# A mixing product of seven by seven block products: when its outer sums and their loads are placed, step by step

## The chip, the cores and the metric

The kernel runs on one core of a Trainium2 chip. TensorE (PE) multiplies, VectorE (DVE) and ScalarE (ACT) work on tiles, GpSimd (POOL) and SyncE (SP) issue DMAs, which 16 DMA engines carry out. The metric is the device time of one execution in microseconds, as the median of several runs.

## The reference

Three networks follow each other; the change lies in the middle one, in the product with `w_spatial`:

```python
h = np.maximum(x @ w_in, 0.0)                     # x: 4 batches, 3072 positions, 256
u, v = h[..., :512], h[..., 512:]
v_n = (v - mean(v)) / np.sqrt(var(v) + 1e-06)
v_s = np.einsum('ts,bsd->btd', w_spatial, v_n) + b_spatial[None, :, None]   # 3072 x 3072
x2 = (u * v_s) @ w_out
r = np.maximum(x2 @ w2_in, 0.0)
out = (s * (r * r) + b) @ w2_out
```

All of it is in float32.

## The kernel before

The program has three stages: `attention`, which also makes `v_n`; `mixing`, which multiplies `w_spatial` with `v_n`; and `output`.

**Products of products.** `mixing` computes a matrix product by Strassen's method in Winograd's form, on two levels. On the outer level there are seven products of a sum of blocks of `w_spatial` (called a) with a sum of blocks of `v_n` (called b). They run in the order of `OUTER`, and are called the first to the seventh outer product here. The second and the fourth have an outer sum on both sides whose result is also kept in DRAM for a later product, the fifth has one on a, the sixth one on both, the seventh one on b; the first and third have none. Each outer product is in turn seven inner products, called passes, in the order of `INNER` (2, 5, 3, 1, 6, 7, 4). A pass has six steps, 0 to 5, one for each strip of 128 rows that are summed over. So an outer product has 42 steps, and the stage 294. A step is 24 matmuls: four groups `d` of 128 columns of b, three products of high and low halves (float32 is split into two parts of fewer bits), two halves of a.

**What stands in memory.** Four quarters of a (`a11`, `a12`, `a21`, `a22`) and of b, each in six strips, have fixed tiles. A quarter of the next outer product is loaded into its tile once the last use of the old one is past (`LAST`, `freed`), on SP's queue. Where the outer product has a sum, the second operand goes into a staging tile, `st_a` or `st_b`, three buffers each, and VectorE adds it (`add`, L786); a result that is kept is stored by a DMA on POOL's queue (L788). A load pair is the tile and its staging tile.

**A step of the program.** The order is written out by hand and each engine works in order. At step n the loop in `run` issues:

- `multiply(n)`, 24 matmuls
- `high` for step n+2: two casts on ScalarE (L845)
- `sums(n + 3)`: the inner sums, on VectorE: none in passes 1, 4 and 7 of the order; one of a and one of b in the second; two of a in the third; three of b in the fifth (L831 to L833); one of a in the sixth (L836). As they are issued three steps ahead, they fall three steps before their pass
- at the last step of a pass `evacuate` for groups 0 and 1: an add of the result to a kept tile on VectorE after passes 4, 5, 6 and 7 (L885, "kept add") and a copy on ScalarE after passes 1, 2, 3 and 6 (L889, "kept copy")
- `low` for step n+2: two subtractions on VectorE (L849), the low halves
- `evacuate` for groups 2 and 3
- outer sums that are due, a conversion if n is in `CONVERSIONS`, and new loads

A group's accumulator has one buffer, so the first matmuls of a pass on it wait until the kept add or copy of the pass before is done.

**Conversions.** Forty times a half of a weight of the last stage, which comes as 64-bit numbers, is converted to two parts: ten operations on VectorE (L143 to L158), one cast on ScalarE (L155) that waits for VectorE's L149, and a store on POOL (L161). They use the same staging buffers: the raw data and the result are `st_a` tiles. The raw data is loaded by SP (L128) ahead of the conversion.

**Before the change** a sum's load is issued as soon as its tile is free and a staging buffer is left (`loads`), and the sum is taken three steps later (`outer_sums(3)`). At a conversion all sums that are open are taken at once (`outer_sums(0)`), so that the staging buffers are free.

Of the kernel before, what the change touches and what calls it, by code (L numbers as in the profile page):

```python
# [27 lines left out]
NS = TQ // 128  # L28
# [140 lines left out]
class Chains:  # L169
# [5 lines left out]
    def add(self, stages):  # L175
        stages[0]()
        rest = list(stages[1:])
        if rest:
            self.live.append(rest)
        return rest  # L180
# [47 lines left out]
def attention(tc, nc, x, w_r, w_i, b_r, b_i, c_f, c_b, c_g, c_v, c_s, zd, vd, yd, vn, chunks, cd, follow, nb=NB):  # L228
# [491 lines left out]
FIRST_USE = {"a12": 0, "b21": 0, "a21": 1, "a22": 1, "b12": 1, "b11": 1, "a11": 2, "b22": 2}  # L720
# [1 line left out]


CONVERSIONS = {42 * g + 6 * p + i for g, p, i in (
# [8 lines left out]


class Stage:
# [6 lines left out]
def mixing(tc, nc, ws, vn, md, sd, convert_half):  # L742
# [10 lines left out]
    def place(pool, names):  # L753
        for name in names:
            n = TQ if name[0] == "a" else 512
            for i in range(NS):
                q[name, i] = pool.tile([128, n], F32, tag=f"{name}{i}", name=name)
# [4 lines left out]
    def source(what, name, i):  # L762

        x, y = int(name[1]) - 1, int(name[2]) - 1
        if what[0] == "w":
            return ws[2 * what[1] + x, (2 * what[2] + y) * NS + i]
        if what[0] == "v":
            return vn[2 * what[2] + y][(2 * what[1] + x) * NS + i]
        return sd[what[0]][x, y, i]

    added = []
    now = [0]

    def load(g, name, i):
        first, then = OUTER[outer[g]][0 if name[0] == "a" else 2:][:2]
        t = q[name, i]
        nc.sync.dma_start(out=t, in_=source(first, name, i))
        if then is None:
            return
        op, second, kept = then  # L780
        n = t.shape[1]
        s = banks[2].tile([128, n], F32, tag="st_" + name[0], name="st_" + name[0], bufs=3)
        nc.sync.dma_start(out=s, in_=source(second, name, i))

        def add():
            nc.vector.tensor_tensor(out=t, in0=t, in1=s, op=getattr(ALU, op))  # L786
            if kept:
                nc.gpsimd.dma_start(out=sd[kept][int(name[1]) - 1, int(name[2]) - 1, i], in_=t)  # L788
        added.append((now[0], name[0], add))

    todo = []

    def loads(taken):

        n = {"a": 3 - taken, "b": 3}
        for _, kind, _ in added:
            n[kind] -= 1
        for x in sorted(todo):
            g, _, i, name = x
            if OUTER[outer[g]][1 if name[0] == "a" else 3] is not None:  # L800
                if n[name[0]] <= 0:
                    continue
                n[name[0]] -= 1
            todo.remove(x)
            load(g, name, i)

    def outer_sums(age):
        while added and added[0][0] <= now[0] - age:
            added.pop(0)[2]()

    sub, add = nc.vector.tensor_sub, nc.vector.tensor_add
    term, hl = {}, {}

    def sums(n):

        p, i = INNER[n // NS % 7], n % NS
        a11, a12, a21, a22, b11, b12, b21, b22 = (q.get((x, i)) for x in QUARTERS)
        if p == 2:
            a, b = a12, b21
        elif p == 5:  # L820
            add(a21, a21, a22)
            sub(b12, b12, b11)
            a, b = a21, b12
        elif p == 3:
            sub(a21, a21, a11)
            a, b = ring.tile([128, TQ], F32, tag="s4", name="s4", bufs=2), b22
            sub(a, a12, a21)
        elif p == 1:
            a, b = a11, b11
        elif p == 6:  # L830
            sub(b12, b22, b12)  # L831
            sub(b11, b12, b11)  # L832
            sub(b22, b21, b12)  # L833
            a, b = a21, b12
        elif p == 7:
            sub(a21, a22, a21)  # L836
            a, b = a21, b11
        else:
            a, b = a22, b22
        term["a", n], term["b", n] = a, b  # L840

    def high(kind, n):
        t = term[kind, n]
        s = hl[kind, n] = ring.tile([128, 2, t.shape[1]], F32R, tag=kind + "_hl", name=kind + "_hl", bufs=3)
        nc.scalar.copy(s[:, 0, :], t)  # L845

    def low(kind, n):
        s = hl[kind, n]
        sub(s[:, 1, :], term.pop((kind, n)), f(s)[:, 0, :])  # L849

    def freed(n):
        g, at = divmod(n // NS, 7)
        if g + 1 < len(outer):
            todo.extend((g + 1, FIRST_USE[x], n % NS, x) for x, last in LAST.items() if last == at)
# [4 lines left out]
    def multiply(n):  # L859
        p, i = INNER[n // NS % 7], n % NS  # L860
        a, b = hl.pop(("a", n)), hl.pop(("b", n))
        fresh = p in (2, 5, 1, 4)
        for d in range(4):
            if i == 0 and fresh:
                acc[d] = banks[0].tile([128, 2, 512], F32, tag=f"acc{d}", name="acc")
            for c, (m, w) in enumerate(PASSES):
                for h in range(2):
                    nc.tensor.matmul(acc[d][:, h, 0:TH], b[:, m, d * 128:(d + 1) * 128], a[:, w, h * TH:(h + 1) * TH],  # L868
                                     start=fresh and i == 0 and c == 0, stop=i == NS - 1 and c == 2,
                                     skip_group_check=True)  # L870
# [6 lines left out]
    def evacuate(n, d):  # L877
        g, at = divmod(n // NS, 7)
        p = INNER[at]
        ps = acc[d][:, :, 0:TH]  # L880
        out = {1: (2, 0, 0), 6: (3, 0, 1), 7: (5, 1, 1), 4: (0, 1, 0)}.get(p)
        if out is not None:
            k, x, y = out
            t = kept.pop((k, d))
            add(t, ps, t)  # L885
            nc.gpsimd.dma_start(out=md[outer[g]][x, y, d], in_=t.rearrange("p h t -> p (h t)"))
        if p in (2, 5, 3, 7):
            t = kept[{7: 0}.get(p, p), d] = keep_tile({2: 0, 5: 1, 3: 2, 7: 0}[p], d)
            nc.scalar.copy(t, ps)  # L889
# [10 lines left out]
    def split_first():  # L900
        n = begun[0]
        begun[0] += 1
        sums(n)
        for kind in "ab":
            high(kind, n)
            low(kind, n)

    def run():
        banks.append(left("m_acc", 1, space=PSUM))
        banks.append(right("m_keep", 1))  # L910
        place(left("m_a11", 1), ("a11",))
        banks.append(left("m_stage", 2))
        stage = banks[2]
        while begun[0] < 2:
            split_first()
        while first:
            _, i, x = first.pop(0)
            load(0, x, i)
        sums(2)
        conversion = []  # L920
        for n in range(total):
            now[0] = n
            multiply(n)
            ends = n % NS == NS - 1
            if n + 2 < total:
                high("a", n + 2)
                high("b", n + 2)
            if n + 3 < total:
                sums(n + 3)
            if ends:  # L930
                evacuate(n, 0)
                evacuate(n, 1)
            if n + 2 < total:
                low("a", n + 2)
                low("b", n + 2)
                freed(n + 2)
            if ends:
                evacuate(n, 2)
                evacuate(n, 3)
            outer_sums(3)  # L940
            if n in CONVERSIONS:
                outer_sums(0)
                conversion.pop()()
            loads(len(conversion))
            if not conversion and any(m in CONVERSIONS for m in range(n + 1, n + 5)):
                conversion.append(convert_half(stage))
        left.close()
        right.close()
# [227 lines left out]
def network(ctx, tc, ins, out):  # L1176
# [25 lines left out]
    with tc.manual_schedule():  # L1202
        attention(tc, nc, ins['x'], ins['w_r'], ins['w_i'], ins['b_r'], ins['b_i'],
                  ins['c_f'], ins['c_b'], ins['c_g'], ins['c_v'], ins['c_s'], zd, vd, yd, vn, chunks, cd,
                  lambda: mixing(tc, nc, ins['moe_w_spatial'], vn, md, sd, convert_half)).run()
        output(tc, nc, yd, md, chunks, cd, ins['moe_b_spatial'], ins['moe2_s'], ins['moe2_b'], out)
# [25 lines left out]
```

## Time and profile before

| | us |
|---|---|
| median of 3 runs | 3177.33 (3176.37 to 3178.32) |
| the profiled execution | 3178.05 |
| its span, first to last instruction | 3176.3 |
| TensorE busy | 3076.6 (97%) |
| VectorE busy | 2309.0 (73%) |
| first and last matmul of `mixing` start at | 539.9 and 1809.9 |

The profile is one execution. The shares are over the whole span. A matmul's record is longer than the time until the next one starts, since matmuls are pipelined; the time of a step is read from the starts of its matmuls. A row of windows below gives the stretch and its length, then busy time and count of PE, PE's weight loads, DVE, ACT and POOL, the granted TensorE clock (1.00 is full speed), the busy share of the DMA engines and the GB/s they moved.

### The profile page before, as it was taken

Reading aid. Unit: us, or ns where it says so; the run is one execution under the profiler, and the core shown is the slowest. Engines: PE = TensorE matmul, PEld = TensorE weight load, DVE = VectorE, ACT = ScalarE, POOL = GpSimd, SP = SyncE. Lnnn points to the kernel's source line nnn. Section 1 sums busy time; section 2 is a strip of 40 time slices with the busy share of each in tenths; the row PEclk is TensorE's granted clock in tenths of the full one; section 3 lists DMA queues with packets and bytes.
Section 4 is the critical chain, followed back from the end, with each engine's and each line's share of the span. In section 5 each row is a group of like instructions: output and inputs, shape, how many; then the busy total and the mean of one; then the engine's idle time right before and its main releaser. Section 6 shows DMA issues by size and latency. Waiting matters only on the chain.

```text
span 3176.3 us, 46578 instructions
## 1 busy us (share of the span) xinstructions
PE 3076.6 (97%) x17960; PEld 3004.5 (95%) x17960; DVE 2309.0 (73%) x3495; ACT 1429.3 (45%) x2244; POOL 420.1 (13%) x537
## 2 busy tenths in 40 slices
PE   6999997999999999999999999999999999999999
PEld 5888986999999899999999989999999999999999
DVE  5888998798878788788888755656565656656564
ACT  5777766433344343434344334444444444444443
POOL 2665534021101200000000100000000000000000
PEclk8999999999999999999999999999999999999999
DMA  8987767586537947375562712111111111110110
GB/s 245 290 285 237 244 215 276 194 337 253 187 138 258 393 147 268 107 258 191 167 211 67 260 63 75 45 45 53 55 65 56 65 56 65 55 65 31 67 45 16
DMA packets 222839, 488.32 MB, mean 154 GB/s; under 512 B 22356, under 2 KB 106136, under 8 KB 222616
## 3 DMA queue, kind: packets, MB, share of 16 engines
q1 hardware_dynamic: 186344, 343.03, 32.0%
q0 software_dynamic: 36272, 142.31, 12.3%
q8 instruction: 141, 2.31, 0.3%
q14 instruction: 82, 0.67, 0.1%
HBM read 322.72 MB, written 162.53 MB: 153 GB/s over the span
## 4 chain that ended last, share of the span: by engine, by line
PE 57%; DVE 5%; ACT 1%; issue 1%; DMA 0%; SPq 0%; ACTq 0%; DVEq 0%
PE ps_h L1073 17%; PE oacc L1094 17%; PE acc L868 15%; PE ps_o L1054 4%; PE ps_u L1036 4%; DVE a_hl L849 1%; DVE kept L885 1%; DVE b_hl L849 1%; DVE b L831 0%; DVE b L833 0%; DVE a L786 0%; DVE b L832 0%; DVE m L1004 0%; ACT kept L889 0%; ACT a_hl L845 0%
## 5 line engine op out<-in xcount | busy, mean ns | idle before, releaser
L868 PE MATMUL acc<-a_hl,b_hl 128*128 128x384 f32 x7056 | 1239.1, 336 | 31.3 <-DVE kept L885 18.1
L868 PEld LDWEIGHTS acc<-a_hl,b_hl 128*128 128x128 f32 x7056 | 1231.4, 189 | 38.9 <-issue 11.0
L1073 PE MATMUL ps_h<-x_hl,w 128*128 128x384 f32 x3072 | 582.4, 337 | 1.5 <-ACT x_hl L1057 0.9
L1094 PE MATMUL oacc<-q_hl,w 128*128 128x384 f32 x3072 | 575.5, 336 | 0.6 <-DVE q_hl L1080 0.6
L1073 PEld LDWEIGHTS ps_h<-x_hl,w 128*128 128x128 f32 x3072 | 544.9, 188 | 2.1 <-ACT x_hl L1057 1.3
L1094 PEld LDWEIGHTS oacc<-q_hl,w 128*128 128x128 f32 x3072 | 537.1, 188 | 0.9 <-DVE q_hl L1080 0.8
L845 ACT CAST a_hl<-a 128x768 fp32r<-128x768 f32 x253 | 211.7, 837 | 512.4 <-PE acc L868 420.2
L1080 DVE TENSOR_TENSOR q_hl<-r,q_hl 128x768 fp32r<-128x768 f32 x256 | 245.4, 959 | 230.7 <-ACT q_hl L1079 230.7
L1078 DVE TENSOR_TENSOR r<-r 128x768 f32<-128x768 f32 x256 | 244.9, 957 | 205.9 <-ACT r L1077 205.9
L1079 ACT CAST q_hl<-r 128x768 fp32r<-128x768 f32 x256 | 213.7, 835 | 301.6 <-DVE r L1078 301.6
L1077 ACT ACTIVATE r<-ps_h 128x768 f32<-128x768 f32 x256 | 208.3, 814 | 312.4 <-PE ps_h L1073 309.1
L849 DVE TENSOR_TENSOR a_hl<-a,a_hl 128x768 fp32r<-128x768 f32 x253 | 241.6, 955 | 126.4 <-ACT a_hl L845 125.8
L849 DVE TENSOR_TENSOR b_hl<-b,b_hl 128x512 fp32r<-128x512 f32 x295 | 202.4, 686 | 0.0
L845 ACT CAST b_hl<-b 128x512 fp32r<-128x512 f32 x295 | 181.7, 616 | 0.1
L578 PE MATMUL ps_vp<-win,y_hl 128*128 128x512 f32 x576 | 149.9, 396 | 1.5 <-ACT y_hl L478 1.2
L1036 PE MATMUL ps_u<-y_hl,w 128*128 128x384 f32 x768 | 145.7, 339 | 1.8 <-DVE y_hl L1022 1.8
L1054 PE MATMUL ps_o<-g,w 128*128 128x384 f32 x768 | 139.4, 337 | 1.6 <-DVE g L1044 1.0
L1036 PEld LDWEIGHTS ps_u<-y_hl,w 128*128 128x128 f32 x768 | 135.5, 190 | 3.1 <-DVE y_hl L1022 2.1
L1054 PEld LDWEIGHTS ps_o<-g,w 128*128 128x128 f32 x768 | 133.6, 188 | 2.5 <-DVE g L1044 1.6
L885 DVE TENSOR_TENSOR kept<-acc,kept 128x768 f32<-128x768 f32 x112 | 103.1, 953 | 23.7 <-PE acc L868 22.4
L578 PEld LDWEIGHTS ps_vp<-win,y_hl 128*128 128x128 f32 x576 | 101.2, 189 | 20.1 <-ACT y_hl L478 1.6
L1043 ACT CAST g<-m 128x768 fp32r<-128x768 f32 x64 | 53.5, 836 | 143.6 <-DVE m L1039 143.6
(140 smaller groups left out, 3722.2 us busy)
## 6 DMA issues: line engine op xcount, KB each, us to landing
a<-in_moe_w_spatial_dram SPq DMA_DIRECT2D x144, 384.0 KB, 4.8
b<-vn SPq DMA_DIRECT2D x168, 256.0 KB, 5.4
md<-kept POOLq DMA_DIRECT2D x112, 384.0 KB, 4.9
m<-md SPq DMA_DIRECT2D x56, 768.0 KB, 6.1
st_a<-in_moe_w_spatial_dram SPq DMA_DIRECT2D x72, 384.0 KB, 6.1
vn<-vr POOLq DMA_DIRECT2D x96, 256.0 KB, 4.5
s<-a POOLq DMA_DIRECT2D x48, 384.0 KB, 6.0
x_f<-in_x_dram SPq DMA_DIRECT2D x32, 384.0 KB, 6.9
```

The lines of the kernel that those rows point to most:

```text
L578: nc.tensor.matmul(ps, y[:, a, k, o:o + 128], win[k][:, w, :], start=c == 0, stop=c == 5)
L845: nc.scalar.copy(s[:, 0, :], t)
L849: sub(s[:, 1, :], term.pop((kind, n)), f(s)[:, 0, :])
L868: nc.tensor.matmul(acc[d][:, h, 0:TH], b[:, m, d * 128:(d + 1) * 128], a[:, w, h * TH:(h + 1) * TH], start=fresh and i == 0 and c == 0, st ...
L1036: nc.tensor.matmul(ps[:, d, 0:TH], win[k][:, a, o:o + 128], y[:, w, k, :], start=c == 0, stop=c == 5)
L1054: nc.tensor.matmul(ps[:, h, 0:TH], wo[k // 2][:, a, o:o + 128], g[:, w, k, :], start=c == 0, stop=c == 11)
L1073: nc.tensor.matmul(ps[:, e, 0:TH], w[:, a, o:o + 128], x[:, i, j, :], start=c == 0, stop=c == 5)
L1077: nc.scalar.activation(r, ps[:, :, 0:TH], AF.Relu)
L1078: nc.vector.tensor_mul(r, r, r)
L1079: nc.scalar.copy(s[:, 0], r)
L1080: nc.vector.tensor_sub(s[:, 1], r, f(s)[:, 0])
L1094: nc.tensor.matmul(ps[:, h, 0:TH], w[:, a, o:o + 128], s[:, i, e, :], start=ff == 0 and c == 0, stop=ff == 2 * NP - 1 and c == 2)
```

## The change

It alters when outer sums, their loads and the conversions are issued; the work itself is the same, operation by operation, and TensorE's order is unchanged.

- Each quarter has a fixed place for its sum, `ADD_AT`, in steps from the start of the outer product ahead of the one that uses it; strip i follows i steps later. 18 is the start of the fourth pass, 30 of the sixth, 36 of the seventh; 42 is the start of the outer product itself, 45 the middle of its first pass and 48 the start of its second.
- A load that belongs to a sum is issued at the earliest `LEAD`, three, steps before that place, if a staging buffer is left.
- At a conversion all open sums are still taken. The table of conversions has 40 other places (a line or two of it is shown); in the second and sixth outer product, for one, they are steps 1 to 4 of the fourth pass.

```diff
 CONVERSIONS = {42 * g + 6 * p + i for g, p, i in (
...
-    (1, 1, 3), (1, 2, 1), (1, 2, 3), (1, 3, 1), (1, 3, 3), (1, 4, 1), (1, 4, 3), (1, 5, 1), (1, 5, 3), (1, 6, 1), (1, 6, 3),
...
+    (1, 2, 1), (1, 2, 4), (1, 3, 1), (1, 3, 2), (1, 3, 3), (1, 3, 4), (1, 5, 1), (1, 5, 3),
+    (1, 6, 1), (1, 6, 2), (1, 6, 3), (1, 6, 4),
...
+ADD_AT = {"a12": 18, "b21": 30, "a21": 36, "b12": 36, "a22": 42, "b11": 42, "b22": 45, "a11": 48}
+LEAD = 3
...
-        added.append((now[0], name[0], add))
+        added.append((g, name, i, add))
...
+    def due(g, name, i):
+        return 42 * (g - 1) + ADD_AT[name] + i
+
     def loads(taken):
 
         n = {"a": 3 - taken, "b": 3}
-        for _, kind, _ in added:
-            n[kind] -= 1
+        for _, name, _, _ in added:
+            n[name[0]] -= 1
         for x in sorted(todo):
             g, _, i, name = x
             if OUTER[outer[g]][1 if name[0] == "a" else 3] is not None:
-                if n[name[0]] <= 0:
+                if n[name[0]] <= 0 or now[0] < due(g, name, i) - LEAD:
                     continue
                 n[name[0]] -= 1
             todo.remove(x)
             load(g, name, i)
 
-    def outer_sums(age):
-        while added and added[0][0] <= now[0] - age:
-            added.pop(0)[2]()
+    def outer_sums(everything=False):
+        for x in list(added):
+            g, name, i, add = x
+            if everything or due(g, name, i) <= now[0]:
+                added.remove(x)
+                add()
+                state[name, i] = g
...
-            outer_sums(3)
+            outer_sums()
             if n in CONVERSIONS:
-                outer_sums(0)
+                outer_sums(True)
                 conversion.pop()()
             loads(len(conversion))
```

**SP's queue, the last b loads of the second outer product.** A row is a line, an operation, what it writes and reads, and the shape; numbers tell tiles apart. The tiles b11_6376 and b22_6341 are the last strip of b11 and the first of b22. Before:

```order
L777 DMA b11_6376<-vn2_71 128x512
L783 DMA st_b_9066<-vn0_69 128x512
L777 DMA a22_6339<-in_moe_w_spatial_dram 128x768
L783 DMA st_a_9103<-in_moe_w_spatial_dram 128x768
L777 DMA b12_6370<-vn3_72 128x512
L783 DMA st_b_9106<-vn1_70 128x512
L777 DMA a22_6340<-in_moe_w_spatial_dram 128x768
L783 DMA st_a_9141<-in_moe_w_spatial_dram 128x768
L777 DMA b22_6341<-vn3_72 128x512
L783 DMA st_b_9180<-vn1_70 128x512
```

And of the change:

```order
L780 DMA b11_6376<-vn2_71 128x512
L787 DMA st_b_9290<-vn0_69 128x512
L780 DMA a11_7547<-in_moe_w_spatial_dram 128x768
L787 DMA st_a_9329<-in_moe_w_spatial_dram 128x768
L780 DMA b22_6341<-vn3_72 128x512
L787 DMA st_b_9332<-vn1_70 128x512
L780 DMA a11_7548<-in_moe_w_spatial_dram 128x768
L787 DMA st_a_9373<-in_moe_w_spatial_dram 128x768
L780 DMA b22_6342<-vn3_72 128x512
L787 DMA st_b_9376<-vn1_70 128x512
L780 DMA b22_6343<-vn3_72 128x512
L787 DMA st_b_9379<-vn1_70 128x512
```

The b22 loads now follow b11's and stand among a11's, which came much earlier before.

**VectorE, around step 4 of the second outer product's first pass.** L786 (L790 after the change) is an outer sum, L821 and L822 (L835 and L836) are the inner sums for the second pass, L849 (L863) the low halves. Before:

```order
L849 TENSOR_TENSOR a_hl_9397<-a21_6359,a_hl_9397 128x768
L849 TENSOR_TENSOR b_hl_9399<-b12_6365,b_hl_9399 128x512
L786 TENSOR_TENSOR b22_6344<-b22_6344,st_b_9301 128x512
L786 TENSOR_TENSOR b22_6345<-b22_6345,st_b_9304 128x512
L821 TENSOR_TENSOR a21_6361<-a21_6361,a22_6337 128x768
L822 TENSOR_TENSOR b12_6367<-b12_6367,b11_6373 128x512
L849 TENSOR_TENSOR a_hl_9433<-a21_6360,a_hl_9433 128x768
L849 TENSOR_TENSOR b_hl_9435<-b12_6366,b_hl_9435 128x512
L786 TENSOR_TENSOR b22_6346<-b22_6346,st_b_9339 128x512
```

And of the change, steps 4 and 5:

```order
L790 TENSOR_TENSOR a22_6339<-a22_6339,st_a_9247 128x768
L790 TENSOR_TENSOR b11_6375<-b11_6375,st_b_9250 128x512
L790 TENSOR_TENSOR b22_6341<-b22_6341,st_b_9332 128x512
L835 TENSOR_TENSOR a21_6361<-a21_6361,a22_6337 128x768
L836 TENSOR_TENSOR b12_6367<-b12_6367,b11_6373 128x512
L863 TENSOR_TENSOR a_hl_9405<-a21_6360,a_hl_9405 128x768
L863 TENSOR_TENSOR b_hl_9407<-b12_6366,b_hl_9407 128x512
L790 TENSOR_TENSOR a22_6340<-a22_6340,st_a_9287 128x768
L790 TENSOR_TENSOR b11_6376<-b11_6376,st_b_9290 128x512
L790 TENSOR_TENSOR b22_6342<-b22_6342,st_b_9376 128x512
L790 TENSOR_TENSOR b22_6343<-b22_6343,st_b_9379 128x512
```

Three and four outer sums now stand in a step where there were two and one, and the first of b22 stands ahead of b11's last.

**ScalarE, the fourth pass of the second outer product.** L845 (L859) are the casts of the high halves, two a step, and L155 is a conversion's cast. Before, the rows from the conversion at step 1 to that at step 3, without the copies at the pass's start:

```order
L155 CAST c_w_9984<-c_w_9982 128x256
L845 CAST a_hl_10023<-a11_7551 128x768
L845 CAST b_hl_10025<-b11_6375 128x512
L845 CAST a_hl_10054<-a11_7552 128x768
L845 CAST b_hl_10056<-b11_6376 128x512
```

And of the change, steps 1 to 3:

```order
L155 CAST c_w_9984<-c_w_9982 128x256
L859 CAST a_hl_10023<-a11_7551 128x768
L859 CAST b_hl_10025<-b11_6375 128x512
L155 CAST c_w_10032<-c_w_10030 128x256
L859 CAST a_hl_10071<-a11_7552 128x768
L859 CAST b_hl_10073<-b11_6376 128x512
L155 CAST c_w_10083<-c_w_10081 128x256
```

Where two steps lay between conversions there is now one.

## Rows read from the trace of the kernel before

**Rows 1.** The page: busy us, share of the span and instructions of each engine.

```profile
PE 3076.6 (97%) x17960; PEld 3004.5 (95%) x17960; DVE 2309.0 (73%) x3495; ACT 1429.3 (45%) x2244; POOL 420.1 (13%) x537
```

**Rows 2.** Instructions on `acc`: shortest, median, longest ns; first and last start, us.

```profile
L868 PE MATMUL acc<-a_hl,b_hl x7056: 333/334/689, 539.9 to 1809.9; 128*128 128x384 f32 x196
L889 ACT COPY kept<-acc x112: 788/802/819, 573.8 to 1787.0; 128x768 f32<-128x768 f32 x112
```

**Rows 3.** Windows cut at step starts: stretch, length, busy time by engine.

```profile
539.88:578.93 39.05, 31.48 (x170) 30.82 (x168) 28.05 (x61) 17.53 (x29) 3.88 (x7) 0.91 0.45 162
687.99:740.37 52.38, 45.16 (x242) 44.56 (x242) 36.54 (x47) 16.66 (x24) 14.61 (x28) 0.93 1.03 414
1050.62:1104.11 53.49, 46.37 (x241) 45.76 (x241) 37.73 (x49) 16.66 (x24) 15.10 (x28) 0.90 1.03 413
1170.67:1207.50 36.83, 34.13 (x193) 33.20 (x193) 31.64 (x52) 15.31 (x24) 3.53 (x6) 1.00 0.69 236
1546.00:1560.57 14.57, 13.05 (x74) 12.44 (x74) 14.36 (x27) 4.38 (x7) 2.85 (x5) 1.00 0.69 241
1723.16:1738.03 14.87, 13.03 (x74) 12.42 (x74) 14.66 (x28) 4.38 (x7) 2.86 (x5) 1.00 0.39 131
...
861.32:866.38 5.06, 4.45 (x25) 4.13 (x25) 5.06 (x7) 1.35 (x2) 2.07 (x4) 1.00 0.84 285
1253.26:1257.77 4.51, 4.45 (x25) 4.13 (x25) 3.77 (x5) 2.86 (x4) 1.09 (x2) 1.00 0.66 243
1054.78:1058.94 4.16, 4.16 (x25) 4.16 (x25) 2.45 (x5) 1.36 (x2) 1.08 (x2) 1.00 1.05 418
```

**Rows 4.** Waits from 687.99 to 740.37: us in total, times, longest us.

```profile
DVE b L786 <- DMA st_b<-vn: 8.4, 7, 3.1
DVE a L786 <- DMA st_a<-in_moe_w_spatial_dram: 7.3, 6, 2.2
...
PE acc L868 <- DVE kept L885: 4.7, 1, 4.7
```

**Rows 5.** DMAs from 680 to 750: traffic; issues, KB each, median us to landing.

```profile
DMA packets 10184, 28.91 MB, mean 413 GB/s; under 512 B 1395, under 2 KB 1395, under 8 KB 10178
...
s<-a POOLq DMA_DIRECT2D x12, 384.0 KB, 6.5
...
st_a<-in_moe_w_spatial_dram SPq DMA_DIRECT2D x10, 384.0 KB, 11.6
...
st_b<-vn SPq DMA_DIRECT2D x14, 256.0 KB, 9.4
```

**Rows 6.** Timeline of VectorE: start us, duration us, instruction; the first to the eleventh follow without gaps.

```profile
852.69 0.95 DVE L849 TENSOR_TENSOR a_hl<-a,a_hl 128x768 fp32r<-128x768 f32 x1
853.56 0.69 DVE L849 TENSOR_TENSOR b_hl<-b,b_hl 128x512 fp32r<-128x512 f32 x1
854.16 0.29 DVE L143 TENSOR_SCALAR c_w<-c_w 128x256 uint32<-128x256 uint32 x1
...
856.76 0.95 DVE L836 TENSOR_TENSOR a<-a,a 128x768 f32<-128x768 f32 x1
```

**Rows 7.** Timeline at the sixth outer product's fourth pass end; in brackets, idle before.

```profile
1551.14 0.41 ACT L155 CAST c_w<-c_w 128x256 fp32r<-128x256 f32 x1 [3.52 <-DVE c_w L149]
...
1551.45 0.83 ACT L845 CAST a_hl<-a 128x768 fp32r<-128x768 f32 x1
...
1552.19 0.61 ACT L845 CAST b_hl<-b 128x512 fp32r<-128x512 f32 x1
...
1558.35 0.98 PE L868 MATMUL acc<-a_hl,b_hl 128*128 128x384 f32 x4 [0.76 <-DVE kept L885]
```

**Rows 8.** DMA issues of the mixing stage, 540 to 1812 (as in rows 5).

```profile
cd<-c_w POOLq DMA_DIRECT2D x40, 256.0 KB, 2.7
...
c_w<-in_moe_w_in_dram SPq DMA_DIRECT2D x20, 256.0 KB, 4.1
```

**Rows 9.** Waits of SP's queue, 540 to 1812: us in total, times, longest us.

```profile
SPq L128 <- DMA cd<-c_w: 138.3, 14, 16.4
```

More of the change, by code (lines that the diff above doesn't have):

```diff
@@ L805, in loads @@
             load(g, name, i)
-    def outer_sums(age):
-        while added and added[0][0] <= now[0] - age:
-            added.pop(0)[2]()
+    def outer_sums(everything=False):
[4 more added lines that the diff above has]
+                add()
+                state[name, i] = g
+    state = {}
     sub, add = nc.vector.tensor_sub, nc.vector.tensor_add
@@ L816, in sums @@
         p, i = INNER[n // NS % 7], n % NS
+        assert all(state[x, i] == n // (7 * NS) for x, use in FIRST_USE.items() if use == n // NS % 7)
         a11, a12, a21, a22, b11, b12, b21, b22 = (q.get((x, i)) for x in QUARTERS)
```

12 rows, old and new, of the table CONVERSIONS are left out of this document.

## The prediction

> **What bounds the kernel now.** The page first: TensorE is busy for 97% of the span [rows 1], so only idle TensorE time can be won. The change touches the mixing stage alone; the rows of its products [rows 2] put it from 539.9 to 1810.2 us (last start plus 0.33), 1270.3 us. A step is 24 matmuls. Undisturbed it takes 4.16 us: the last row of [rows 3] is one step (25 matmuls are counted because one overlaps the edge). 294 steps would take 1223 us, so about 47 us are lost, 1.5% of the span. That is the most any order of this work can win here.
>
> Next, windows cut at step starts show where [rows 3]. In each, the time over 4.16 us a step is the loss:
> - start of the stage, 7 steps: 39.05 - 29.1 = 9.9
> - crossing from the first to the second outer product, 10 steps: 52.38 - 41.6 = 10.8; from the third to the fourth, the same steps: 53.49 - 41.6 = 11.9
> - fourth outer product, 8 steps around the end of its third and fourth pass: 36.83 - 33.3 = 3.5
> - end of the fourth pass in the sixth outer product, 3.5 steps: 14.57 - 12.5 = 2.1; in the seventh: 14.87 - 12.5 = 2.4
> - first step of the sixth pass, 5.06 - 4.16 = 0.9, in five of the seven outer products, so 4.4; first step of the seventh pass, 4.51 - 4.16 = 0.34, in the five that are not within a crossing's window, so 1.7.
> These make 46.7.
>
> Then the waits of the first crossing [rows 4]: VectorE waits for staged loads (8.4 and 7.3 us), and TensorE for VectorE's kept adds (4.7 at once). VectorE runs in order, so an outer sum whose load is late holds up the kept adds and the low halves behind it. The loads are late because the DMA engines are full: 413 GB/s for 70 us, staged loads landing 9.4 to 11.6 us after issue while the stores that share the engines take 6.5 [rows 5]. In the two crossings the granted clock is 0.93 and 0.90 on average, 1.00 in the other windows of the running stage [rows 3]: behind its long idle times TensorE ran for a while at the lower of its two levels, 1.2 and 2.4 GHz, and that loss is inside the windows.
>
> The other losses are VectorE's own queue. Back to back it spends 0.87 us on a tile of a, 0.60 on one of b and 2.60 on a conversion (854.16 to 856.76) [rows 6]. A step needs the two low halves, 1.47; three b sums add 1.8, a kept add 0.87. Whatever exceeds 4.16 a step becomes lag, and at the end of a pass with kept adds there is almost no slack: TensorE starts the next pass only when the third kept add is done [rows 7].
>
> **What the change removes.** No outer sum falls into the fifth pass and, but for one in the seventh outer product, no conversion. VectorE then needs 3.3 us or less in most of its steps and enters the last one without lag: the five losses of 0.9 go, 4.4. Sums are no longer forced at a conversion right after their load was issued; that is the fourth outer product's 3.5. The small queue losses at the fourth pass (2.1, 2.4) and both crossings (22.7) are replaced by the following.
>
> **What it adds at the two crossings.** Here I add up bytes. A pair of loads is 768 KiB for a, 512 for b; a kept result's store 384 or 256; the four stores at the end of a pass 1536. The engines move 413 GB/s, or 404 KiB/us, 1680 a step. By the new order, counted in steps of the outer product ahead (35 ends its sixth pass, 42 is the next one's first): step 35 asks for 3072, 36 to 40 for 1920 each, 41 for 3456, 42 to 45 for 1920, 46 for 2688, 47 for 3456. The engines are full from about 2 us into step 35 until all of that has moved. The sums of a11 and b22 come late in the new order, and three slots for b must serve b11 and b22 in the same steps: SyncE's order above has the first b22 load behind b11's last, and VectorE's has that b22 sum before b11's last. So its load is issued one step ahead, not three, and the next two likewise.
>
> The first b22 load lies behind 23,808 KiB, 58.9 us. With 2 us for the start, 2 for landing (a 256 KiB store on idle engines takes 2.7 [rows 8], of which 0.6 are its bytes) and 1.5 off for stores still in flight, it lands 61.4 us after step 35 began. Step 46 begins after 45.8, so VectorE stands until 15.6 us into it; then the sum, 0.6, and two sums and low halves for step 49, 2.9: 19.1. Step 49 should begin 12.5 after step 46: 6.6 lost. The next two, 2688 KiB or 6.7 us later, make step 50 late by 9.7 in all; the fourth, 5 us more, step 51 by 10.6. From there VectorE needs 4.4 us a step against 4.16 for two steps, 0.5; and ScalarE's kept copies at the end of the second pass start 0.7 late. Together 11.8, twice 23.6. Below lies the case that TensorE loses nothing until the third b22 sum and stores trail more, 8; above, one more slow clock stretch and loads that miss their turn, 15.
>
> At the crossing into the sixth outer product nothing is stored for keeping: 1280 KiB a step, under 1680. Before lost nothing there but the 0.34; the late b22 pairs cost 0.3 (0 to 3).
>
> The Trainium skill ("DMA: Bandwidth & Descriptors", Specifications) gives a core about 358 GB/s of HBM. By it the 30.7 MB that steps 35 to 47 ask for would take 85.7 us, not 74.3, and each crossing would lose 11.4 us more. The rows say 413 over 70 us [rows 5], so the row is used.
>
> **What it adds elsewhere.**
> - Four conversions stand at steps 1 to 4 of the fourth pass in the second and sixth outer products (ACT's order above). The seventh outer product of before had them at 1, 2 and 4 there and lost 2.4; VectorE was not idle between, so one more at step 3 adds 2.6: 5.0 each, less 0.1 of slack, 9.8. The seventh now has 1, 3 and 4, where less lag drains: 2.8. Sum 12.6 (9 to 15).
> - The third outer product has conversions at steps 1 to 4 of its first pass. ScalarE's one cast of a conversion (L155) waits for VectorE's L149 [rows 7]; VectorE's lag is 2.8 at step 4 (two steps of 2.6 + 1.47 + 1.47 against 4.16). Undisturbed its low halves end 2.6 us into a step (a cast of 0.83, then 0.95 and 0.69 [rows 6]); L149 comes 1.4 later, the cast takes 0.41, so it ends 3.1 us into step 5. There two casts of halves (0.83 and 0.61 [rows 7]) and a copy of 0.80 [rows 2] follow, and TensorE waits for the copy 1.2. The same four at the end of the second outer product: 0.4.
> - The seventh pass keeps its 0.34, also at the two crossings: 0.7 more outside the terms above.
> - Four conversions in a row reuse the staging buffers: a load waits until the store of the conversion but one before has landed. 2.7 and 4.1 us [rows 8] with 2.6 of VectorE are 9.4 for two steps of 8.3. I take 0, as the lag of the fourth pass hides most; the upper end is 1.1 a pair, eight pairs, 9.
>
> **Sum.** Removed: 4.4 + 3.5 + 22.7 + 2.1 + 2.4 = 35.1. Added: 23.6 + 0.3 + 12.6 + 1.2 + 0.4 + 0.7 = 38.8. Net +3.7. The profiled execution took 3178.05 us, its span 3176.3 and 1.75 around it; it lies 0.7 over the median of the runs, 3177.33. So 3177.33 + 3.7, about **3181 us**. The start's 9.9 stays: its first conversion has not moved.
>
> **Rivals.**
> - The crossings get cheap (faster). If staged loads are served ahead of stores, the loads of steps 35 to 45, 14,080 KiB, need 35 us and no sum is late; if half so, a crossing loses 5: 13.6 less, 3167. It decides where the first b22 load lands within 9 us of step 46's start. For it: sums are spread over 36 steps, and nothing is forced. Against: in the full stretch the stores are the quick ones [rows 5]. Chance 0.17.
> - The conversions in a row wait for their buffers (slower). At 1.1 us a pair, or with a lag that reaches into the next pass: 8 more, 3189. SyncE's loads of conversions already wait 138.3 us for stores, though mostly off the path [rows 9]. It decides where VectorE stands at L143 for over 1 us in steps 3 and 4. Chance 0.2.
> - The traffic is held under 413 GB/s (slower). A tenth less is 8.2 us more for the 30.7 MB, 16 at two crossings, 3197. No row shows less while the engines are full: 0.02. By the Trainium skill's figure above it would be 23 more, 3204.
> - The forecast, 0.55, by itself 3174 to 3187; the rest, 0.06, lies about it without a cause I can name.
>
> **Range and chances.** 0.2%, 6.4 us, is about what a measurement of this kernel can tell from no change. My case gives same 0.38 and slower 0.17; the cheap crossings faster 0.17; the buffers slower 0.16, same 0.04; less traffic slower 0.02; the rest 0.02, 0.04, 0. That is faster 0.19, same 0.46, slower 0.35. The range 3167 to 3190 leaves out half of the cheap crossings, a third of the buffers' case and the last one.
>
> **What would show it.** In the profile after: no loss at the first step of the sixth pass; the fourth outer product's wait gone; DMA at 413 GB/s from the end of the sixth pass until well into the second outer product, with VectorE standing for b22's staged loads and one long TensorE idle near its step 7; about 5 us at the end of the fourth pass in the second and sixth outer products. Wrong, if the first b22 load there lands in under 8 us, if TensorE runs through the crossing, or if VectorE waits at L143.

## The result and the profile after

The changed kernel takes 3201.04 us (median of 6 runs, 3196.15 to 3204.09) against 3177.82 for the kernel before in the same comparison (6 runs, 3176.37 to 3179.78): a ratio of 1.0072, 95% interval 1.0059 to 1.0085. It is slower by 23 us. The prediction, 3181 with a range of 3167 to 3190, was wrong: slower had been given a chance of 0.35, but the time lies beyond the range.

The profiled execution took 3199.22 us, 21.2 more than that of before. On the page TensorE is busy 7.5 us longer than before [rows 1], and its work is the same; the rest is waiting:

```profile
PE 3084.1 (96%) x17960; PEld 3005.4 (94%) x17960; DVE 2306.1 (72%) x3495; ACT 1426.8 (45%) x2244; POOL 420.2 (13%) x537
```

The mixing stage now runs from 540.1 to 1830.0 us, 1289.9 for 1270.3: 19.6 of the 21.2 are in it. Windows cut at step starts of the changed kernel, columns as in [rows 3] (stretch, length, busy time of PE, PEld, DVE, ACT and POOL, granted clock, DMA share, GB/s):

```profile
540.14:579.19 39.05, 32.25 (x170) 31.60 (x169) 28.09 (x61) 17.61 (x28) 3.88 (x7) 0.91 0.47 169
699.83:818.83 119.00, 106.18 (x577) 102.92 (x577) 94.06 (x134) 42.36 (x63) 24.57 (x45) 0.94 0.89 334
1076.65:1193.39 116.74, 104.70 (x577) 100.40 (x577) 89.53 (x116) 41.95 (x61) 23.20 (x43) 0.97 0.87 331
839.63:852.68 13.05, 8.88 (x50) 8.27 (x49) 12.88 (x25) 2.91 (x5) 2.85 (x6) 1.00 0.55 184
1566.40:1580.87 14.47, 11.04 (x49) 10.75 (x49) 14.30 (x27) 2.91 (x5) 2.87 (x6) 0.76 0.55 200
1747.60:1758.82 11.22, 8.86 (x49) 8.25 (x49) 11.05 (x22) 3.02 (x5) 2.85 (x5) 1.00 0.51 175
919.57:929.90 10.33, 8.89 (x50) 8.28 (x49) 9.63 (x19) 2.92 (x5) 3.18 (x6) 1.00 0.64 211
946.54:956.02 9.48, 8.63 (x50) 8.31 (x50) 9.38 (x19) 5.71 (x9) 0.68 (x1) 1.00 0.35 112
1514.40:1524.80 10.40, 9.14 (x49) 8.20 (x49) 10.33 (x14) 6.68 (x10) 0.00 (x0) 1.00 0.34 105
674.87:679.03 4.16, 4.16 (x26) 4.16 (x26) 4.16 (x6) 1.36 (x2) 1.08 (x2) 1.00 0.64 247
1189.23:1222.51 33.28, 33.28 (x193) 33.28 (x193) 26.01 (x35) 13.85 (x20) 2.16 (x4) 1.00 0.41 131
1268.27:1272.77 4.50, 4.45 (x26) 4.12 (x26) 2.90 (x4) 2.85 (x4) 1.08 (x2) 1.00 0.94 335
```

Row by row, less 4.16 us a step:

| stretch | steps | predicted loss | measured |
|---|---|---|---|
| start | 7 | 9.9 | 9.9 |
| seventh pass to third pass, first to second outer product | 24 | 12.1 | 19.2 |
| the same, third to fourth | 24 | 12.1 | 16.9 |
| end of the fourth pass, second outer product | 2 | 4.9 | 4.7 |
| the same, sixth | 2 | 4.9 | 6.1 |
| the same, seventh | 2 | 2.8 | 2.9 |
| end of the second outer product | 2 | 0.4 | 2.0 |
| end of the third one's first pass | 2 | 1.2 | 1.2 |
| end of the sixth one's second pass | 2 | 0.3 | 2.1 |
| first step of the sixth pass | 1 | 0 | 0 |
| fourth outer product | 8 | 0 | 0 |
| first step of the seventh pass | 1 | 0.34 | 0.34 |

(12.1 is the 11.8 of a crossing and the seventh pass's 0.34.) Between these rows every step takes 4.16 us, but for 0.34 in each of the other seventh passes, so the first step of the sixth pass loses nothing in any outer product. The loss sits where it was expected and nearly everywhere with the expected size. The two crossings alone are 12 us over, the sixth outer product 3, the end of the second 1.6.

### The profile page after: what moved, and what is told of

Read it like the earlier page. It is cut to its first block, busy times and chain, and to the rows that moved or that the text cites. A ratio compares the mean times of both kernels' runs of the same rounds, so it can differ in the third digit from the quotient of the medians.

```text
span 3197.5 us, 46549 instructions
## 1 busy us (share of the span) xinstructions
PE 3084.1 (96%) x17960; PEld 3005.4 (94%) x17960; DVE 2306.1 (72%) x3495; ACT 1426.8 (45%) x2244; POOL 420.2 (13%) x537
## 4 chain that ended last, share of the span: by engine, by line
PE 77%; DVE 12%; DMA 6%; ACT 3%; issue 2%; SPq 0%; ACTq 0%; DVEq 0%
PE acc L882 28%; PE ps_h L1087 17%; PE oacc L1108 16%; PE ps_o L1068 4%; PE ps_u L1050 4%; PE ps_m L413 3%; DMA st_b<-t 2%; DMA st_b<-vn 1%; PE ps_vp L578 1%; DVE a_hl L863 1%; PE ps_z L339 1%; PE ps_g L366 1%; DVE b_hl L863 1%; DVE bn L591 1%; DVE kept L899 1%
## 5 line engine op out<-in xcount | busy, mean ns | idle before, releaser
L859 ACT CAST a_hl<-a 128x768 fp32r<-128x768 f32 x253 | 211.6, 836 | 555.5 <-PE acc L882 403.0
L863 DVE TENSOR_TENSOR a_hl<-a,a_hl 128x768 fp32r<-128x768 f32 x253 | 241.3, 954 | 142.7 <-ACT a_hl L859 142.4
L863 DVE TENSOR_TENSOR b_hl<-b,b_hl 128x512 fp32r<-128x512 f32 x295 | 201.9, 685 | 0.0
L859 ACT CAST b_hl<-b 128x512 fp32r<-128x512 f32 x295 | 181.6, 616 | 0.0
L900 POOL DMA_DIRECT2D md<-kept x112 | 60.6, 541 | 434.0 <-DVE kept L899 433.5
```

## Experiments

**Theory.** In a crossing the DMA engines are full; a staged load that is late stops VectorE, which works in order, and TensorE stops for the low halves and kept adds queued behind. So the loss follows the rate at which bytes are asked for, and the step at which a late sum stands in VectorE's queue. **Rival 1:** VectorE's own work there is more than a step holds, whatever the loads do. **Rival 2:** the conversions cause the rise.

Results of all runs; "crossings" are the windows of 24 steps (seventh pass and the next three) less 99.84 us, "fourth pass" the windows of two steps at its end in the second, sixth and seventh outer product less 8.32. A ratio is to the runs of the kernel before in the same comparison, whose medians are 3177.8 to 3179.5:

| kernel | us, median | ratio to before (95%) | crossings | fourth pass |
|---|---|---|---|---|
| before | 3177.82 | | 8.1, 9.8 | 0.3, 2.1, 2.4 |
| the change | 3201.04 | 1.0072 (1.0059 to 1.0085) | 19.2, 16.9 | 4.7, 6.1, 2.9 |
| sums_alone | 3201.47 | 1.0067 (1.0052 to 1.0082) | 25.4, 17.4 | 0.3, 2.1, 2.1 |
| conversions_alone | 3187.65 | 1.0027 (1.0018 to 1.0036) | 8.1, 8.2 | 5.2, 6.4, 2.9 |
| no_kept_stores | 3167.17 | 0.9956 (0.9941 to 0.9971) | 2.8, 1.4 | 6.4, 5.2, 2.9 |
| before_no_kept_stores | 3155.52 | 0.9921 (0.9907 to 0.9935) | 0.4, 0.4 | 0.3, 2.1, 2.1 |
| b22_at_48 | 3178.83 | 0.9996 (0.9986 to 1.0005) | 9.5, 8.8 | 6.1, 4.7, 2.9 |
| b_slots_apart | 3188.36 | 1.0025 (1.0014 to 1.0037) | 14.2, 11.9 | 5.1, 5.3, 2.9 |
| spread_sums | 3184.99 | 1.0017 (1.0008 to 1.0026) | 8.3, 9.4 | 5.3, 5.2, 2.9 |
| spread_both | 3165.58 | 0.9951 (0.9937 to 0.9965) | 9.4, 9.4 | 0.3, 0.3, 0.3 |
| spread_later | 3148.35 | 0.9907 (0.9891 to 0.9924) | 0.3, 0.3 | 0.3, 0.3, 0.3 |

(The cuts of [rows 3] take in the three steps ahead of these windows, where the kernel before lost 2.7 and 2.6 more. 12.1 was predicted for each crossing of the change, 4.9, 4.9 and 2.8 for its fourth passes.)

**1. Which half of the change.** The two halves apart.

```diff
 # sums_alone: ADD_AT and LEAD as in the change
-CONVERSIONS = (those of the change)
+CONVERSIONS = (those of before)
 # conversions_alone: the kernel before
-CONVERSIONS = (those of before)
+CONVERSIONS = (those of the change)
```

Expected of the sums: 

> The changed kernel's outer sums with the conversions at the steps of before. If the sums cause the loss (late second operands of b22 behind full DMA engines), the two crossings stay near the 35.2 us that they lost in the changed kernel, against 22.7 before, and the end of the fourth pass falls back to some 2.4 us in the second and sixth outer products (4.7 and 6.1 in the changed kernel): 3190 to 3196. If the conversions cause most of the rise, this kernel lies within 6 us of before: 3172 to 3184.

Expected of the conversions: 

> The kernel before with the conversions at the changed kernel's steps. If the sums cause most of the loss, the crossings stay at some 23 us, four conversions in a row cost 2.5 to 4 us at the end of the fourth pass of the second and sixth outer products and 1 to 2 at two later ends, and some of the 0.9 of the sixth pass goes: 3177 to 3186. If the conversions are the cause, 3190 or more. Sums are still forced at a conversion, so the fourth outer product's wait can move rather than go.

Measured: 3201.47 and 3187.65. The sums alone give all of the rise, 5 us above what was expected, and their first crossing is dearer still: before's conversions have one at step 51, in the middle of it, and behind it TensorE waits 4.7 us for a kept copy, where the change waits 0.5.

The conversions alone cost 8.9 us, 1.7 above the upper end of what was expected. The ends of the fourth pass lose 9.7 more than before, the crossings lose no more than before, and other places give a little back. So the halves don't add: against sums_alone the change loses 9 us more at the fourth passes and 7 less in the crossings, which its conversions stand clear of. Rival 2 falls for the crossings.

**2. Loads or VectorE's work.** The kept stores left out, in the change and in the kernel before.

```diff
-    5: (("w", 1, 0), ("add", ("w", 1, 1), "s1"), ("v", 0, 1), ("subtract", ("v", 0, 0), "t1")),
+    5: (("w", 1, 0), ("add", ("w", 1, 1), None), ("v", 0, 1), ("subtract", ("v", 0, 0), None)),
...
-    6: (("s1",), ("subtract", ("w", 0, 0), "s2"), ("v", 1, 1), ("subtract", ("t1",), "t2")),
-    3: (("w", 0, 1), ("subtract", ("s2",), None), ("v", 1, 1), None),
+    6: (("w", 1, 0), ("subtract", ("w", 0, 0), None), ("v", 1, 1), ("subtract", ("v", 0, 1), None)),
+    3: (("w", 0, 1), ("subtract", ("w", 1, 1), None), ("v", 1, 1), None),
...
-    4: (("w", 1, 1), None, ("v", 1, 0), ("subtract", ("t2",), None)),
+    4: (("w", 1, 1), None, ("v", 1, 0), ("subtract", ("v", 0, 0), None)),
```

Expected of the change: 

> The sums of the second and fourth outer products are not stored for later use, and what later reads them reads weights or values of the same size instead, so the products of the third to seventh outer product are other ones; loads, sums, products and their order stay. Of 30.7 MB asked for in 13 steps of a crossing 8.5 fall away. If full DMA engines make the loads late, a crossing loses at most 4 us in place of 18.7 and 16.5: 3168 to 3178. If VectorE's own queue makes them late, it still loses 10 or more each: 3187 or more.

Expected of the kernel before: 

> The kernel before with its kept stores left out in the same way (the products of the third to seventh outer product are other ones). If its 22.7 us at the two crossings come from full DMA engines too, they fall to 4 or less together: 3157 to 3163. If they come from VectorE's queue of sums and kept adds at those steps, 15 or more stay: 3170 or more.

Measured: 3167.17, 34 less than the change, and 3155.52, 24 less than before; they lie 0.8 and 1.5 us below the lower end of what was expected. The crossings of the change without these stores, with the same 134 VectorE instructions in the first:

```profile
701.74:804.41 102.67, 101.35 (x577) 99.55 (x577) 93.61 (x134) 42.56 (x63) 4.60 (x8) 1.00 0.75 264
1063.50:1164.71 101.21, 100.42 (x577) 99.78 (x577) 88.64 (x116) 42.15 (x61) 3.23 (x6) 1.00 0.73 259
```

VectorE is busy for 93.6 us in place of 94.1, and 16.3 of the 19.2 are gone. Rival 1 falls: the work very nearly fits, if the operands are there. In both kernels the loss of a crossing needs the bytes of these stores. How much is lost for the same bytes is the next question.

**3. Where b22 stands.** One number changed, and then two others.

```diff
 # b22_at_48
-ADD_AT = {..., "b12": 36, "a22": 42, "b11": 42, "b22": 45, "a11": 48}
+ADD_AT = {..., "b12": 36, "a22": 42, "b11": 42, "b22": 48, "a11": 48}
 # b_slots_apart
-ADD_AT = {..., "b12": 36, "a22": 42, "b11": 42, "b22": 45, "a11": 48}
+ADD_AT = {..., "b12": 33, "a22": 42, "b11": 39, "b22": 45, "a11": 48}
```

Expected: 

> Only b22's steps change, from 45 to 50 to 48 to 53, so that its loads no longer share steps and staging with those of b11 and are issued three steps ahead. If VectorE stands for b22's staged load in the middle of work that TensorE needs sooner, the 10.7 and 9.4 us at the second step of the second pass fall below 3, some of it comes back two or three steps later, and the crossings lose 20 in place of 35: about 3186. If VectorE is late by its own work (4.9 to 6.3 us of sums and low halves a step there), the crossings stay above 30: 3196 or more.

Expected: 

> b22's sums stay where the changed kernel has them (steps 45 to 50); those of b12 and b11 go three steps earlier, to 33 and 39, so that no two blocks of b want the three staging slots in the same steps and b22's loads are issued three steps ahead instead of one. The bytes of a crossing stay and are asked for a little earlier. If the one step of lead is what made b22's sums late, the 10.7 and 9.4 us at the second step of the second pass fall below 3 and the crossings lose 12 or less in place of 35: 3175 to 3182. If the backlog of bytes alone sets it, the loads only queue for longer and the crossings still lose 25 or more: 3190 or more.

Measured: 3178.83 and 3188.36. With b22 three steps later, 22 us are gone, 7 more than expected. VectorE's wait for staged loads in the first crossing, of the change and then of b22_at_48 (us in total, times, longest):

```profile
DVE b L790 <- DMA st_b<-vn: 16.2, 6, 8.7
...
DVE a L790 <- DMA st_a<-in_moe_w_spatial_dram: 3.0, 1, 3.0
```

```profile
DVE b L790 <- DMA st_b<-vn: 6.9, 8, 2.2
DVE a L790 <- DMA st_a<-in_moe_w_spatial_dram: 2.8, 1, 2.8
```

The long wait of 8.7 is gone. The bytes are the same; b22's sums now stand behind the low halves and sums of three more steps. So the bytes alone don't set the loss: with the same bytes the two crossings lose 18 us in place of 36. With b12 and b11 three steps earlier and b22 left at 45, b22's loads also get three steps of lead in the program, and no wait of TensorE is left at the second step of the second pass (in the first crossing it runs for 23.0 us without a stop from that pass's start); but the crossings still lose 14.2 and 11.9, over two thirds. VectorE waits as long (13.0 in 8 and 5.9 in 2, longest 5.7), at other steps, some of it now ahead of the kept adds at the end of the seventh pass. 12 or less together was expected if the lead alone counted, 25 or more if the bytes did. It measured 26, so the lead alone is not the cause, though the time, 3188.36, lies between the two ranges that were expected. The 10 us less than the change come with the longer lead and with the earlier places of b12's and b11's sums; this run does not separate the two.

**4. Asking for the bytes earlier, and later.** The same rule and code; only the table of steps, and then the conversions (the lines taken out are not shown, nor is spread_both's own table of conversions, which like spread_later's has only steps 1 and 3 in the fourth pass of the second, sixth and seventh outer product).

```diff
 # spread_sums, spread_both
-ADD_AT = {"a12": 18, "b21": 30, "a21": 36, "b12": 36, "a22": 42, "b11": 42, "b22": 45, "a11": 48}
+ADD_AT = {"a12": 15, "a11": 20, "b21": 26, "a21": 31, "b12": 32, "a22": 37, "b11": 38, "b22": 43}
 # spread_later
+ADD_AT = {"a12": 15, "a11": 20, "b21": 25, "a21": 31, "b12": 32, "b11": 38, "a22": 42, "b22": 46}
+CONVERSIONS = {42 * g + 6 * p + i for g, p, i in (
+    (0, 1, 1), (0, 1, 3), (0, 2, 0),
+    (1, 1, 4), (1, 2, 1), (1, 2, 3), (1, 3, 1), (1, 3, 3), (1, 4, 0), (1, 4, 3), (1, 5, 1), (1, 5, 3), (1, 6, 1), (1, 6, 3),
+    (2, 0, 1), (2, 0, 3), (2, 1, 1), (2, 1, 3), (2, 2, 0),
+    (3, 1, 3), (3, 2, 0), (3, 4, 2),
+    (4, 1, 0), (4, 1, 2), (4, 1, 4), (4, 2, 0),
+    (5, 1, 3), (5, 2, 1), (5, 2, 3), (5, 3, 1), (5, 3, 3),
+    (6, 1, 4), (6, 2, 0), (6, 2, 2), (6, 2, 4), (6, 3, 1), (6, 3, 3), (6, 4, 3), (6, 5, 1), (6, 5, 3))}
```

Expected of spread_sums: 

> All outer sums of a crossing spread over steps 15 to 48 in place of 18 to 53, one block of a and one of b at a time, as early as their tiles come free; conversions at the changed kernel's steps. By bytes the backlog then peaks at some 13 us in place of 20 and no load has less than its three steps. If late loads are the cause, a crossing loses 4 or less in place of 18.7 and 16.5, the ends of the fourth pass keep their 4.7, 6.1 and 2.9, and forced sums cost up to 3 in the fourth outer product: 3166 to 3176. If b22's place alone counts, a crossing still loses 8 to 9 as with b22 at 48: 3178 or more.

Expected of spread_both: 

> The same sums, and the conversions taken out of the last steps ahead of kept adds, never at consecutive steps and where no sum is open. By the theory that VectorE's backlog ahead of the kept adds and late loads are all that is lost, the start's 8 to 10 us and some 6 us elsewhere remain of the changed kernel's 66: 3150 to 3160. If the conversions' places don't matter, it equals the kernel with the sums spread alone.

Expected of spread_later: 

> The spread order again, with a22 five steps later (37 to 42), b22 three steps later (43 to 46), b21 one earlier, and the conversions moved so that none falls on open sums but two of b22. In the first spread order 1920 KiB were asked for in each of steps 31 to 39, and VectorE stood for late loads ahead of the kept adds at the end of the seventh pass, where 9 us a crossing were lost. If the rate at which bytes are asked for sets the loss, the crossings now lose under 3 each and the whole falls by 10 to 14 more: 3150 to 3157. If kept adds at the end of the seventh pass are late for another reason, 3162 to 3166 as before it.

Measured: 3184.99, 3165.58 and 3148.35. The first two missed their expectations by 9 and 6 us, mainly for one reason: 8 to 9 us a crossing stayed. For spread_sums that is the number that had been expected if b22's place alone counted; the place decides against it, as the loss is no longer at step 49 but at the end of the seventh pass. In spread_both VectorE stands there for late sums of a, right ahead of the kept adds (its timeline, in brackets the idle time before; then TensorE's longest wait of that crossing):

```profile
725.02 0.96 DVE L790 TENSOR_TENSOR a<-a,st_a 128x768 f32<-128x768 f32 x1 [2.61 <-DMA st_a<-in_moe_w_spatial_dram]
...
729.65 0.96 DVE L790 TENSOR_TENSOR a<-a,st_a 128x768 f32<-128x768 f32 x1 [1.59 <-DMA st_a<-in_moe_w_spatial_dram]
730.52 1.81 DVE L899 TENSOR_TENSOR kept<-acc,kept 128x768 f32<-128x768 f32 x2
...
PE acc L882 <- DVE kept L899: 5.2, 1, 5.2
```

That is the theory in another place, so the last kernel moved a22 from step 37 to 42, behind that pass end, b22 three steps later, b21 one earlier, and conversions with them. Its crossings lose 0.3 each, and it is 1.7 us faster than the lower end of what was expected. Its windows, crossings first, then the ends of the fourth pass:

```profile
699.76:799.93 100.17, 100.12 (x578) 99.80 (x577) 85.72 (x129) 43.22 (x64) 17.69 (x32) 1.00 0.75 281
1052.16:1152.33 100.17, 100.12 (x578) 99.80 (x577) 85.85 (x123) 42.94 (x63) 17.01 (x31) 1.00 0.76 285
820.73:829.36 8.63, 8.62 (x49) 8.30 (x49) 8.56 (x13) 2.71 (x4) 2.19 (x4) 1.00 0.66 226
1525.69:1534.30 8.61, 8.60 (x49) 8.28 (x49) 8.54 (x13) 2.71 (x4) 2.18 (x4) 1.00 0.72 256
1701.03:1709.63 8.60, 8.59 (x49) 8.27 (x49) 8.53 (x13) 2.71 (x4) 2.17 (x4) 1.00 0.44 165
```

Both crossings run through with all the kept stores in place, at a granted clock of 1.00. It beats the kernel before by 29.8 us (0.9907, 0.9891 to 0.9924) and the change by 52.7. How differently the bytes flow is seen in windows of 20 us, of the change and then of spread_later:

```profile
680.00:700.00 20.00, 20.00 (x118) 20.00 (x116) 13.39 (x19) 7.65 (x12) 3.78 (x7) 1.00 0.89 295
...
740.00:760.00 20.00, 16.12 (x86) 14.23 (x84) 12.54 (x17) 5.50 (x8) 3.78 (x7) 1.00 1.04 412
760.00:780.00 20.00, 11.57 (x52) 10.84 (x53) 14.17 (x20) 4.06 (x6) 3.78 (x7) 0.74 0.98 349
780.00:800.00 20.00, 19.55 (x104) 19.23 (x103) 19.86 (x26) 8.23 (x12) 3.78 (x7) 0.91 0.84 293
```

```profile
680.00:700.00 20.00, 20.00 (x117) 20.00 (x117) 17.45 (x23) 7.59 (x12) 5.40 (x10) 1.00 1.03 411
...
740.00:760.00 20.00, 20.00 (x117) 20.00 (x116) 19.15 (x27) 9.77 (x14) 3.78 (x7) 1.00 0.91 340
760.00:780.00 20.00, 20.00 (x118) 20.00 (x117) 19.45 (x31) 9.34 (x14) 1.75 (x3) 1.00 0.42 135
780.00:800.00 20.00, 20.00 (x117) 20.00 (x117) 14.88 (x31) 9.05 (x15) 1.36 (x2) 1.00 0.39 124
```

The last kernel has moved most of its bytes by 760; the change still moves 349 GB/s from 760 to 780 and 293 from 780 to 800. With the same sums, spread_both against spread_sums also shows the price of the conversions' places: the ends of the fourth pass go from 5.3, 5.2 and 2.9 to 0.3 each when the conversions stand at steps 1 and 3 in place of 1 to 4 (1, 3 and 4 in the seventh outer product).

## Why the prediction was wrong

**Right.** What the change removes: the five losses of 0.9 and the fourth outer product's 3.5 are gone, and the start's 9.9 stays. The kinds of loss it adds, and their places: b22's loads, issued late behind full engines, one long wait near step 7, VectorE's backlog at the fourth pass (4.7 and 2.9 for 4.9 and 2.8), the third outer product's first pass (1.2).

**The step that failed** is the sum's largest term, 11.8 for a crossing. The mechanism held; the size was 18.8 and 16.6, beyond the 15 that was its upper end. For the first crossing, in the order of its working:

- *"It lands 61.4 us after step 35 began."* It landed 67.4 after: step 35 began at 695.67, and VectorE could add at 763.12. The timelines of SyncE (the issue of b22's first staged load) and of VectorE:

```profile
753.49 0.33 SPq L787 DMA_DIRECT2D st_b<-vn  x1
```

```profile
763.12 0.69 DVE L790 TENSOR_TENSOR b<-b,st_b 128x512 f32<-128x512 f32 x1 [8.74 <-DMA st_b<-vn]
763.73 0.95 DVE L835 TENSOR_TENSOR a<-a,a 128x768 f32<-128x768 f32 x1
```

  SP's queue had held the load back: from 735 to 754 it stood 13.2 us (4.6, 3.3, 2.7 and 2.6, by kind of load) until earlier loads had landed, so a lead counted in steps of the program was not a lead at the engines. In those 67.43 us 399 GB/s moved (first row below), 26,270 KiB, where the prediction had counted 23,808 ahead of the load: 2,460 KiB too few, 6.1 us. I had treated the engines as one line in which nothing overtakes and which is empty at the start. The load took 9.6 us from issue to landing, while requests issued after it moved too (a store of a sum issued at 754.07 landed after 5.9), and at 690 to 695.67 the engines were already busy with older requests. How the 2,460 KiB split between the two stays open.
- *Only b22 was counted as late.* The sums ahead of it, with three steps of lead (12.5 us), were late as well: between 730 and 755 VectorE stood 3.0 for a staged a and 4.6, in three waits, for staged b. Steps 46 to 48 lost 3.1 us (second row) where the sum had nothing. Two of these waits:

```profile
737.00 0.96 DVE L790 TENSOR_TENSOR a<-a,st_a 128x768 f32<-128x768 f32 x1 [2.97 <-DMA st_a<-in_moe_w_spatial_dram]
740.83 0.69 DVE L790 TENSOR_TENSOR b<-b,st_b 128x512 f32<-128x512 f32 x1 [2.87 <-DMA st_b<-vn]
```

- *Step 49 lost 6.6, step 50 3.1 more, step 51 0.9 more.* TensorE waited 8.4, 0 and 2.2: the second and third b22 loads were there when their sums came up, 4.4 us after the first, the fourth was not. TensorE's waits at steps 49 and 51:

```profile
PE acc L882 <- DVE a_hl L863: 8.4, 1, 8.4
...
PE acc L882 <- DVE a_hl L863: 2.2, 1, 2.2
```

- *The granted clock was not in the term.* Behind the two waits it was 0.65 and 0.80 (third and fourth row), so the work of one step, 4.16, took 14.82 - 8.4 = 6.4 and 8.49 - 2.2 = 6.3: 4.4 more.

```profile
695.67:763.10 67.43, 60.39 (x339) 58.18 (x338) 45.38 (x59) 23.53 (x34) 16.73 (x31) 0.98 1.03 399
741.76:757.32 15.56, 13.85 (x74) 12.28 (x73) 11.61 (x16) 5.50 (x8) 3.78 (x7) 1.00 1.04 412
757.32:772.14 14.82, 6.44 (x25) 6.02 (x25) 9.02 (x13) 2.71 (x4) 2.70 (x5) 0.65 0.97 344
776.30:784.79 8.49, 6.27 (x25) 5.64 (x25) 8.49 (x13) 2.71 (x4) 1.62 (x3) 0.80 1.03 378
```

3.1 + 8.4 + 2.2 + 4.4, and some 0.7 at the end of the second pass (as the sum had it), make the 18.8. The second crossing is alike: 7.9 of wait at its step 49, 16.6 in all.

**Smaller terms.** The crossing into the sixth outer product, 0.3 predicted with 3 as its upper end, lost 2.1; VectorE waited once for a staged b, 2.6 us between 1455 and 1521, and with more than 4.16 us of work a step from there on it did not catch up before the kept copies. With b22 at 48 nothing is lost there. At the end of the second outer product 2.0 in place of 0.4: VectorE waited there 2.6 us, in three waits, for conversions' loads at L143, as the buffers' rival had it; no run tests this one. In the whole stage such waits make 6.1. The sixth outer product's fourth pass lost 6.1 for 4.9: behind its idle time TensorE ran at the lower clock, as the last section shows.

**The rivals.** "Held under 413 GB/s" fell where the loss arises: 412 in the second row above. The 399 over all 67.43 us falls short of 413 by 2.4 us of time, about what the sum had set aside for the start. But its "No row shows less while the engines are full" was a misreading (last section). The Trainium skill's 358 GB/s for a core's HBM ("DMA: Bandwidth & Descriptors", Specifications), which by the prediction's estimate would have given 3204, near the measured 3201, is not why. The Trainium skill's "Perfetto Trace Analysis" (Roofline) says that one core alone may pull more than that share, up to some 435 GB/s of its 16 DMA engines. The rows agree, with 412 and 413 GB/s. "Staged loads served ahead of stores" fell with the 8.7 us wait. The buffers' rival gave 3189; by the trace it holds for at most 1.6 us at one place.

## What to carry to other kernels

When an order moves loads, add up bytes asked for per step against what the engines move, for every load in the full stretch and not only for the one with the shortest lead; a lead in steps does not make a load timely once the backlog is longer than the lead (sums with three steps of lead were late here). On an engine that works in order, a late operand costs what stands behind it: put such a sum after the work that the bottleneck needs next, and keep it away from the last steps ahead of kept adds (one number of the table was worth 22 us here, the table and the conversions 52.7). And price a wait of several us at the bottleneck above its length: behind both waits of the first crossing the work ran at the lower clock and added 2 us each time.

## What was not expected of the hardware

Busy DMA engines don't always move the same: from 690 to 715 us the share was 1.01 at 369 GB/s, from 715 to 760 it was 1.03 at 413. The kernel before had shown this too, with 383 at 1.03 late in the fifth outer product (last row). What makes the difference was not settled.

```profile
690.00:715.00 25.00, 24.94 (x144) 24.62 (x143) 18.71 (x26) 11.24 (x16) 7.02 (x13) 1.00 1.01 369
715.00:760.00 45.00, 41.12 (x230) 39.23 (x228) 29.44 (x39) 13.65 (x20) 10.79 (x20) 1.00 1.03 413
...
1418.00:1446.00 28.00, 27.95 (x162) 27.63 (x161) 24.07 (x32) 11.55 (x17) 2.16 (x4) 1.00 1.03 383
```

And two idle times of the same length did not cost the same. At the end of the fourth pass TensorE stood for 3.41 us in the second outer product and went on at full clock; in the sixth it stood for 3.43, and 25 matmuls then took 7.05 us, 282 ns each:

```profile
847.37 2.35 PE L882 MATMUL acc<-a_hl,b_hl 128*128 128x384 f32 x12 [3.41 <-DVE kept L899]
```

```profile
1574.16 7.05 PE L882 MATMUL acc<-a_hl,b_hl 128*128 128x384 f32 x25 [3.43 <-DVE kept L899]
```

The granted clock of those windows is 1.00 and 0.76, and in b22_at_48, with idle times of 3.41 and 3.40, it is the other way round (6.1 lost in the second, 4.7 in the sixth). Behind the wait of only 2.2 us at step 51 of the crossing the clock fell as well, to 0.80 over wait and step. So the length of an idle time alone did not decide it; what did was not settled.
